# Centred rows for the first two token blocks of a sliding-attention and gMLP kernel

## The chip, the cores and the metric

The kernel runs on one core of a Trainium2 chip. A core has five engines, each with its own queue of instructions: TensorE (PE in the profile; its weight loads are PEld), VectorE (DVE), ScalarE (ACT), GpSimd (POOL) and SyncE (SP), which here only issues transfers. SP's, ScalarE's and GpSimd's queues issue DMAs; 16 DMA engines carry them out. The metric is the device time of one execution, in microseconds (us); the median of several runs counts.

## The reference

`x` holds 2048 tokens of 512 numbers. The rows are normalised once, `xn = (x - mean) / sqrt(var + 1e-5)`, and two mixers work on `xn`; their results are added to `x`.

```python
# A: dilated sliding attention, 32 heads of 16, window of 8 tokens, 2 apart
q, k, v = split(xn @ wqkv)
logits = einsum('bhsd,bhswd->bhsw', q, k[s - 2*w]) * 16**-0.5
a = softmax(logits) . v[s - 2*w] @ wo
# B: a gated MLP that mixes tokens
z = gelu(xn @ w_in)                       # 1792 wide
z1, z2 = z[..., :896], layernorm(z[..., 896:])
g = w_sp @ z2 + b_sp                      # w_sp: 2048 x 2048 over tokens
b = (z1 * g) @ w_out
return x + a + b
```

Types are bfloat16, with sums in float32.

## The kernel before

The tokens lie in 16 blocks of 128. A block has its tokens on the 128 partitions when it is loaded (`ldx`, tile `xin`, 8 slots), and its features on the partitions after it has been normalised and transposed (`xnT`), which is the form in which TensorE takes it as the stationary or the moving operand.

The work is a list of named tasks. A task is one or a few instructions on one engine, with the tiles that it reads and writes; from these the program derives the semaphore waits. The order of the tasks on each engine is not computed when the kernel is built: it is written out by hand in the five lists of `ORDERS` (line 206), and every engine runs its list strictly in order. A number behind a name is the token block, or the pair of blocks, or a group of columns.

How a block is made ready (`ln_block`, line 591):

- `bnst`, `bnag` (DVE, L595 and L598): mean and variance of the rows, from the loaded block.
- `rstd` (POOL, L600): variance to the power -0.5, a 128x1 operation.
- `norm` (DVE, L602): subtract the mean and multiply by `rstd`, written as `xn` in four slots.
- blocks 0 to 3: `xTr`, four 128x128 matmuls against the identity (PE, L619) into PSUM, and `xTe` (ACT, L633), which copies them to `xnT`. For block 0 the copy is split between ACT (`xTe0`, L625) and DVE (`xTf0`, L629).
- blocks 4 to 15: `xTd`, a transposing DMA on SP's queue (L606).

Before there is any work for it, TensorE runs filler matmuls on zeros: nine 128x512 ones (`warm`, L567), and two 128x320 ones behind xTr0 (`fill0`).

Then, on TensorE: `z2_b_h` (L815), the second half of `xn @ w_in` for block b, in two halves h of 448 columns (their weights are `w_in2a` and `w_in2b`, each loaded in two parts, one by SP's and one by ScalarE's queue); for blocks 0 to 3 it comes first of all. `z2g` (ACT, L826) is the gelu of a block, which also gives the sum of each row, and `z2s` (L834) the sum of squares; `zn` (L863, or L859 on ACT) normalises the block by them once four blocks are there. `Qj_c` and `Kj_c` (L669) are made for four blocks j at once, so that Q0_0 needs `xnT` of blocks 0 to 3 and the loaded weights `ldq`; K0_0 needs `ldk`; `V` (L646) needs `ldwv`. `QKe` and `Ve` (ACT) evacuate them.

The logits are products on DVE (`prod`, `padd`, L694 and L698, 128x4096 each), summed over the head's features on TensorE (`lg`, L707); the softmax follows, and later the products with V (`pv`, `pva`, `pvc`, L1000 to L1008). In between TensorE makes `z1` (L815). Then follow, for eight pairs of token blocks, the token mixing `w_sp @ z2` (`P1` to `P7`, L938; sums of weight blocks `S13`, `S2`, `S4` and of z2 blocks `T1` to `T4` on DVE save one product in eight), its evacuation, the gate `u` (DVE, L970), a transposing DMA of the result (`uT`, L980) and one of the attention's output (`OTd`, L1012), and the output product `out` (L1037 and L1041), which is added to x in PSUM, copied (`fin`) and stored (`st`).

PSUM has eight banks. Banks 0 to 5 go round in pairs through the products before the token mixing: a pair is written again when its evacuation is done.

The queue of SP begins with `ldx0 ldw_in2a_0 ldx2 ldw_in2b_0 ldx4 ldx5 ldx8 ldx6 ldx7 ldq ldx9 ldk ldx10 ldx11 ldwv xTd5`. Block 8 and those behind it are loaded into the slots of blocks 0 and on, so such a load waits until the old block has been read.

Of the kernel before, what the change touches and what calls it, by code (L numbers as in the profile page):

```python
# [14 lines left out]
class Plan:  # L15
# [183 lines left out]
ALU = mybir.AluOpType  # L199
# [8 lines left out]
warm xTr0 fill0 z2_0_0 xTr1 z2_0_1 z2_1_0 xTr2 z2_1_1 z2_2_0 xTr3 z2_2_1 z2_3_0 z2_3_1 Q0_0 Q0_1 K0_0 K0_1 K0_2  # L208
Q0_2 Q0_3 V0 V1 V2 V3 V6 K0_3 Q1_0 K1_0 V7 V4 V5 K1_3 Q1_3 Q1_1 Q1_2 K1_2 K1_1 z2_6_0 z2_6_1 z2_5_0 z2_4_1
z2_4_0 z2_5_1 lg0_0 z2_7_0 z2_7_1 V11 V10 V9 Q2_0 V8 K2_0 Q2_2 K2_1 Q2_1 K2_2 K2_3 Q2_3 z2_8_0 z2_8_1 z2_9_0  # L210
z2_10_0 z2_10_1 z2_9_1 z2_11_1 z2_11_0 V12 V13 lg1_0 Q3_0 K3_0 Q3_1 V14 K3_1 V15 K3_3 Q3_3 Q3_2 z2_12_1 K3_2
z2_14_1 z2_14_0 z2_12_0 z2_13_0 z2_13_1 lg2_0 z2_15_0 z2_15_1 z1_0_1 z1_2_0 z1_4_0 z1_4_1 z1_0_0 z1_2_1 z1_10_1
z1_6_1 z1_6_0 z1_8_1 z1_10_0 z1_8_0 z1_12_0 z1_12_1 z1_15_1 z1_15_0 z1_13_0 z1_13_1 z1_9_0 z1_9_1 lg3_0 z1_14_0
z1_7_0 z1_7_1 z1_14_1 z1_3_1 z1_1_1 z1_1_0 z1_11_1 z1_3_0 z1_11_0 P5_0 P1_1 z1_5_0 z1_5_1 P1_0 P5_1 P3_0 P6_0
P2_0 P7_0 P6_1 P4_0 P7_1 P2_1 P4_1 P1_2 P3_1 P2_2 P5_2 P6_2 P1_3 P3_2 P7_2 P2_3 P4_2 P6_3 P5_3 out0_0 P1_4 P7_3
P3_3 P4_3 P6_4 out2_0 P2_4 P5_4 P7_4 P3_4 P4_4 P1_5 out4_0 out6_0 P2_5 P1_6 P6_5 P5_5 P7_5 out8_0 out10_0 P3_5
P2_6 P5_6 P4_5 out12_0 out14_0 P6_6 P1_7 P3_6 P5_7 P7_6 P2_7 out15_0 P6_7 P4_6 P7_7 P3_7 out13_0 out11_0 P4_7
out9_0 out7_0 out5_0 out3_0 out1_0 out1_1
# [6 lines left out]
QKe3_0 QKe3_1 Ve15 Ve14 QKe3_3 z2s10 z2s11 QKe3_2 z2g14 z2g12 bspf z2g13 z2s12 z2g15 ldV0_0 lge2 z1g4 z1g0 z1g2
z2s13 z1g6 z2s14 z1g10 z2s15 z1g12 zm2 z1g15 z1g13 z1g8 lge3 z1g9 z1g7 z1g14 zn14 z1g1 zn13 z1g3 zn12 z1g11 zn15
S5_0 z1g5 fk_0 sexp0 fk_1 S2e_0 ldxr0 Sc_0 sln0 S3e_0 srec0 S2e_1 g11_0 g22_0 S5_1 g12_0 g21_0 S3e_1 g11_1 fk_2
sexp1 g21_1 Sc_1 S5_2 g22_1 S2e_2 os0_0 fk_3 sln1 ldxr2 Sc_2 S3e_2 g12_1 srec1 g21_2 os2_0 g11_2 S2e_3 S5_3
ldxr4 g22_2 ldV1_7 fin0_0 S3e_3 fk_4 g12_2 Sc_3 ldxr6 fin2_0 g11_3 S2e_4 g12_3 S5_4 g21_3 os4_0 st0_0 S3e_4
# [14 lines left out]
T1_1 zn10 T1_0 zn11 T3_0 S4_0 sm1_0 sm2_0 sm3_0 ssub0 S2_1 T3_1 T2_1 T2_0 T4_1 S4_1 sz1_0 sz2_0 sz3_0 T4_0 sm1_1
sm2_1 sm3_1 ssub1 h_0 sattn0 pv0 pv2 pva2048_0 S13_2 sz1_1 S2_2 sz2_1 h_1 pva1024_0 S4_2 pvc0 sz3_1 S13_3 u_0
S2_3 pv4 pv6 h_2 S4_3 sattn1 u_4 pva2048_1 S13_4 pva1024_1 S2_4 pvc1 S4_4 pv10 pv8 h_3 pva2048_2 pva1024_2 u_8
pvc2 S13_5 pv14 pv12 S2_5 pva2048_3 pva1024_3 h_4 pvc3 u_12 pv15 pv13 S4_5 pva2048_4 S13_6 pva1024_4 u_15 pvc4
h_5 pv11 pv9 S2_6 pva2048_5 pva1024_5 S4_6 pvc5 S13_7 pv5 S2_7 pv7 h_6 pva2048_6 u_11 pva1024_6 S4_7 pvc6 pv1
# [8 lines left out]
ldx13 Vw0 Vw1 Vw2 ldx12 ldx15 Vw3 xTd10 Vw7 xTd8 xTd9 Vw6 xTd11 Vw5 Vw4 ldw_in1 Vw8 xTd15 Vw10 xTd13 Vw11 xTd12  # L257
Vw9 xTd14 wT1_0 wT1_1 wT0_0 Vw12 Vw15 wT0_1 Vw14 Vw13 lgT1 lgT0 lgT3 lgT2 wT2_0 wT2_1 wT3_0 wT3_1 OTd0 uT_0
wT4_0 wT4_1 uT_2 uT_4 uT_6 wT5_0 OTd1 wT5_1 wT6_0 wT6_1 OTd2 uT_8 uT_10 OTd3 wT7_0 uT_14 uT_12 OTd4 wT7_1 uT_15
uT_13 OTd5 uT_11 OTd6 uT_9 uT_7 uT_5 uT_3 OTd7 uT_1 st1_0  # L260
# [6 lines left out]
    warm=9,  # L267
# [11 lines left out]
def build_kernel(nc, A_x, A_wqkv, A_wo, B_x, B_w_in, B_w_sp, B_b_sp, B_w_out, out,   # L279
# [49 lines left out]
    off["pb"] = base  # L329
    off["On"] = base  # L330
# [31 lines left out]
    with ExitStack() as es:  # L362
# [75 lines left out]
        for c in range(4):  # L438
# [749 lines left out]
```

## Time and profile before

| what | value |
|---|---|
| median of 3 runs | 226.94 us (226.94 to 227.38) |
| the profiled execution | 227.02 us, its span 225.2 us |
| TensorE busy | 220.5 us, 98% of the span |
| VectorE busy | 203.4 us, 90% |
| ScalarE busy | 148.5 us, 66% |
| GpSimd busy | 42.9 us, 19% |
| first useful matmul (`z2_0_0`) | 6.43 us after the span's start |
| Q and K begin | 13.69 us (first record) |
| last matmul ends | 222.9 us |

A line of the timeline gives the start, the duration of the merged group in us, the engine, the line of the kernel, the operation, its output and input, the count, and in brackets the idle time of the engine before the group and what ended it. A line of the groups gives the busy time and the mean duration of one instruction in ns. The time of an execution is the span and some 1.8 us around it.

### The profile page before, as it was taken

Reading aid. Unit: us, or ns where it says so; the run is one execution under the profiler, and the core shown is the slowest. Engines: PE = TensorE matmul, PEld = TensorE weight load, DVE = VectorE, ACT = ScalarE, POOL = GpSimd, SP = SyncE. Lnnn points to the kernel's source line nnn. Section 1 sums busy time; section 2 is a strip of 40 time slices with the busy share of each in tenths; the row PEclk is TensorE's granted clock in tenths of the full one; section 3 lists DMA queues with packets and bytes.
Section 4 is the critical chain, followed back from the end, with each engine's and each line's share of the span. In section 5 each row is a group of like instructions: output and inputs, shape, how many; then the busy total and the mean of one; then the engine's idle time right before and its main releaser. Section 6 shows DMA issues by size and latency. Waiting matters only on the chain.

```text
span 225.2 us, 3059 instructions
## 1 busy us (share of the span) xinstructions
PE 220.5 (98%) x1129; PEld 115.8 (51%) x1142; DVE 203.4 (90%) x208; ACT 148.5 (66%) x258; POOL 42.9 (19%) x40
## 2 busy tenths in 40 slices
PE   7999999999999999999999999999999999999995
PEld 3454454455454677665555554545454545544443
DVE  4879999999999999998699999999999999999700
ACT  2678767898969797897895686434525824546652
POOL 3438804990603205006000000000000000000000
DMA  6975536225925370451989189997898977347862
GB/s 207 347 191 86 173 74 171 111 71 135 232 80 140 89 260 0 91 98 43 237 120 212 45 173 160 302 236 181 172 129 238 182 159 137 96 111 175 189 148 70
DMA packets 84719, 34.18 MB, mean 152 GB/s; under 512 B 69232, under 2 KB 84352, under 8 KB 84704
## 3 DMA queue, kind: packets, MB, share of 16 engines
q1 hardware_dynamic: 74448, 23.77, 50.2%
q10 hardware_dynamic: 9376, 8.75, 13.2%
q0 software_dynamic: 880, 1.47, 2.4%
q8 instruction: 9, 0.15, 0.3%
q14 instruction: 6, 0.05, 0.1%
HBM read 12.98 MB, written 4.21 MB: 76 GB/s over the span
## 4 chain that ended last, share of the span: by engine, by line
PE 98%; issue 0%; DVE 0%
PE ps L938 38%; PE ps L815 22%; PE ps L669 12%; PE ps L1041 11%; PE ps L646 6%; PE ps L1037 6%; PE ps L567 2%; PE ps L707 1%; PE ps L619 0%; DVE arena L629 0%; DVE arena L1049 0%; DVE arena L493 0%; DVE fpool L494 0%
## 5 line engine op out<-in xcount | busy, mean ns | idle before, releaser
L938 PE MATMUL ps<-arena 128*128 128x448 bf16 x448 | 86.2, 352 | 0.0
L938 PEld LDWEIGHTS ps<-arena 128*128 128x128 bf16 x448 | 43.8, 98 | 41.3 <-ACT arena L944 0.4
L815 PE MATMUL ps<-arena 128*128 128x448 bf16 x256 | 50.8, 353 | 0.4 <-DVE arena L629 0.4
L815 PEld LDWEIGHTS ps<-arena 128*128 128x128 bf16 x256 | 30.2, 121 | 19.2 <-ACT arena L633 1.1
L694 DVE TENSOR_TENSOR arena<-arena 128x4096 bf16<-128x4096 bf16 x16 | 36.3, 2284 | 0.1
L1000 DVE TENSOR_TENSOR arena<-arena 128x4096 bf16<-128x4096 bf16 x16 | 36.1, 2288 | 0.1
L826 ACT ACTIVATE arena<-ps 128x896 bf16<-128x896 f32 x32 | 28.8, 915 | 7.7 <-PE ps L815 7.6
L669 PE MATMUL ps<-arena 128*128 128x512 bf16 x125 | 28.8, 379 | 0.2
L944 ACT ACTIVATE arena<-ps 128x448 bf16<-128x448 f32 x32 | 17.0, 542 | 17.7 <-PE ps L938 16.5
L1004 DVE TENSOR_TENSOR arena<-arena 128x4096 bf16<-128x4096 bf16 (+1 forms) x16 | 28.1, 1756 | 0.1
L600 POOL TENSOR_TENSOR fpool<-fpool 128x1 f32<-128x1 f32 x16 | 24.0, 1507 | 20.3 <-DVE fpool L598 19.3
L698 DVE TENSOR_TENSOR arena<-arena 128x4096 bf16<-128x4096 bf16 x12 | 27.4, 2285 | 0.1
L1041 PE MATMUL ps<-arena 128*128 128x512 bf16 (+2 forms) x117 | 26.9, 366 | 0.1
L1050 ACT ACTIVATE arena<-ps 128x512 bf16<-128x512 f32 (+1 forms) x16 | 9.5, 592 | 21.5 <-PE ps L1041 21.5
L669 PEld LDWEIGHTS ps<-arena 128*128 128x128 bf16 x128 | 14.4, 113 | 13.4 <-issue 0.4
L677 ACT ACTIVATE arena<-ps 128x1024 bf16<-128x1024 f32 x16 | 16.4, 1033 | 6.3 <-PE ps L669 6.2
L1041 PEld LDWEIGHTS ps<-arena 128*128 128x128 bf16 x119 | 11.4, 98 | 12.8
L851 POOL TENSOR_TENSOR fpool<-fpool 128x4 f32<-128x4 f32 x4 | 12.1, 3022 | 28.7 <-DVE fpool L848 28.7
L1037 PE MATMUL ps<-arena 128*128 128x512 bf16 (+2 forms) x62 | 15.3, 365 | 0.3
L834 ACT ACTIVATE arena<-arena 128x896 bf16<-128x896 bf16 x16 | 15.3, 954 | 0.1
L646 PE MATMUL ps<-arena 128*128 128x512 bf16 x62 | 14.5, 379 | 0.1
L595 DVE BATCH_NORM_STATS2 fpool<-arena 128x6 f32<-128x512 bf16 x16 | 10.6, 680 | 2.8 <-DMA arena<-in_A_x_dram 2.8
(76 smaller groups left out, 186.0 us busy)
## 6 DMA issues: line engine op xcount, KB each, us to landing
arena<-in_A_x_dram ACTq DMA_DIRECT2D x18, 128.0 KB, 2.8
vscr<-arena SPq DMA_DIRECT2D x16, 128.0 KB, 1.9
arena<-vscr ACTq DMA_DIRECT2D x1, 1920.0 KB, 9.0
out_dram<-arena ACTq DMA_DIRECT2D x15, 128.0 KB, 2.6
arena<-in_A_x_dram SPq DMA_DIRECT2D x14, 128.0 KB, 3.5
arena<-in_A_wqkv_dram SPq DMA_DIRECT2D x3, 512.0 KB, 5.0
arena<-vscr ACTq DMA_DIRECT2D x1, 1024.0 KB, 6.9
arena<-in_B_w_in_dram SPq DMA_DIRECT2D x1, 896.0 KB, 5.1
```

The lines of the kernel that those rows point to most:

```text
L600: T("pool", lambda g: g.tensor_tensor(Fv("rstd", 1, b), Fv("mv", 1, 2 * b + 1), Fv("mhalf", 1), ALU.pow), reads=[("mv", b), "mhalf"], writ ...
L646: last = t.matmul(bank(k + i), AC(off["xnT"] + dc * S + 128 * (b + i), [[1, 128]]), AC(off["wv_raw"] + 512 * dc, [[1, 512]]), start=(dc == ...
L669: last = t.matmul(bank(k + which), AC(off["wqk"] + 1024 * dc + col0, [[4, 128]]), AC(off["xnT"] + dc * S + 512 * j, [[1, 512]]), start=(dc ...
L694: T("dve", lambda v: v.tensor_tensor(pbv, qb, kb, ALU.mult), reads=[("QT", c, j), ("KT", c, j), ("KTpad", c, j)], writes=[("pb", s_)], est ...
L698: T("dve", lambda v: v.tensor_tensor(A("pb", 4096, 4096 * a), A("pb", 4096, 4096 * a), A("pb", 4096, 4096 * b), ALU.add), reads=[("pb", b) ...
L815: last = t.matmul(bank(k + hf, HF), AC(off["xnT"] + dc * S + t0, [[ts, 128]]), AC(off["w_in"] + 1792 * dc + c0, [[1, HF]]), start=(dc == 0 ...
L826: T("act", lambda a: a.activation(A(nm, FH, FH * b).rearrange("p (t n) -> p t n", t=2), PC(512 * k, [[512, 2], [1, HF]]), ACTF.Gelu_apprx_ ...
L938: last = t.matmul(bank(k, HF), AC(lo + 128 * s, [[1, 128]]), mov(s), start=(first and s == 0), stop=(s == 7), skip_group_check=True)
L1000: T("dve", (lambda iv, tv, av: lambda v: v.tensor_tensor(tv, iv, av, ALU.mult))(iv, tv, av), reads=[("attn", pairs[i][b]) for b in blks] + ...
L1004: T("dve", (lambda n: lambda v: v.tensor_tensor(AC(off["Vs"], [[4096, 2], [1, n]]), AC(off["Vs"], [[4096, 2], [1, n]]), AC(off["Vs"] + n, ...
L1037: t.matmul(po, AC(off["OT"] + 512 * os_ + 128 * cc, [[1, 128]]), AC(off["wo"] + 512 * cc + c0, [[1, n]]), start=False, stop=False, skip_gr ...
L1041: last = t.matmul(po, AC(off["uT"] + FH * us + 128 * fc, [[1, 128]]), AC(off["w_out"] + 512 * fc + c0, [[1, n]]), start=False, stop=(fc == ...
```

## The change

For token blocks 0 and 1, z2 is no longer computed from the normalised rows but from centred ones, `xc = x - mean`. The product of the weights with `xc` is multiplied by `rstd` inside the gelu instruction, whose scale operand is then the block's `rstd` (a number for each partition, that is, for each token).

- Block 0: `cen0` (DVE) subtracts the mean as soon as `bnag0` has given it. Block 1: `sum1` (ACT) computes minus the mean by an accumulating copy, and `cen1` (ACT) adds it, without DVE's statistics.
- `xTr0` and `xTr1` transpose `xc`, and `xTe0`, `xTf0`, `xTe1` copy it to a tile of its own, `xcT`. `xTr1` stands directly behind `xTr0` on TensorE, ahead of `fill0` and `z2_0_0`; the order behind that is z2_0_0, z2_1_0, z2_0_1.
- The full norms of blocks 0 and 1 (`norm0`, `norm1`) are still needed for Q, K, V and z1. They are transposed by two DMAs on SP's queue, `xTd0` and `xTd1`, which stand behind `ldx7`.
- `ldq` moves from SP's queue to ScalarE's, behind `xTe1`; `ldx8` moves behind `ldk`, which is behind `xTd1`.
- `warm` has eight matmuls instead of nine; `fill0` is 256 wide instead of 320.
- All five lists of `ORDERS` are new, to the end. They hold the same tasks as before but for those named.

```diff
     pe="""
-warm xTr0 fill0 z2_0_0 xTr1 z2_0_1 z2_1_0 xTr2 z2_1_1 z2_2_0 xTr3 z2_2_1 z2_3_0 z2_3_1 Q0_0 Q0_1 K0_0 K0_1 K0_2
-Q0_2 Q0_3 V0 V1 V2 V3 V6 K0_3 Q1_0 K1_0 V7 V4 V5 K1_3 Q1_3 Q1_1 Q1_2 K1_2 K1_1 z2_6_0 z2_6_1 z2_5_0 z2_4_1
...
+warm xTr0 xTr1 fill0 z2_0_0 z2_1_0 z2_0_1 xTr2 z2_1_1 z2_2_0 xTr3 z2_2_1 z2_3_0 z2_3_1 Q0_0 Q0_1 Q0_2 K0_0 K0_2
+K0_1 K0_3 Q0_3 V1 V2 V0 V3 V4 V7 Q1_0 V5 V6 K1_0 Q1_1 K1_1 Q1_3 K1_3 Q1_2 K1_2 z2_6_0 z2_4_1 z2_4_0 z2_5_0
...
     act="""
-actprime ldx1 ldw_in2a_1 ldw_in2b_1 ldx3 xTe0 xTe1 z2g0 xTe2 z2g1 xTe3 z2s0 z2g2 z2g3 QKe0_0 QKe0_1 halo0_0
...
+actprime ldx1 ldw_in2a_1 ldw_in2b_1 ldx3 sum1 cen1 xTe0 xTe1 ldq xTe2 z2g0 xTe3 z2g1 z2g2 z2g3 QKe0_0 halo0_0
...
     dve="""
-zeros steps0 steps1 bnst0 bnag0 bnst1 norm0 bnag1 xTf0 norm1 bnst2 bnag2 norm2 bnst3 bnag3 bnst5 bnag5 norm3
-bnst7 bnst6 bnst8 norm5 bnag6 bnst10 bnag7 bnst4 bnag10 bnst9 bnag4 zq0 bnst11 norm6 norm7 bnag8 prod0_0 norm4
...
+zeros steps0 steps1 bnst0 bnag0 cen0 bnst1 bnag1 xTf0 norm0 bnst2 bnag2 norm1 norm2 bnst3 bnag3 bnst5 bnag5
+norm3 bnst7 bnag7 bnst4 bnst6 norm5 bnst8 bnag4 bnag8 norm7 norm4 bnst9 bnag6 bnst11 bnag9 prod0_0 norm6 bnag11
...
     sp="""
-ldx0 ldw_in2a_0 ldx2 ldw_in2b_0 ldx4 ldx5 ldx8 ldx6 ldx7 ldq ldx9 ldk ldx10 ldx11 ldwv xTd5 xTd6 xTd7 ldx14 xTd4
...
+ldx0 ldw_in2a_0 ldx2 ldw_in2b_0 ldx4 ldx5 ldx6 ldx7 xTd0 xTd1 ldk ldx8 ldx9 ldx11 ldx10 ldwv xTd5 xTd7 ldx13
...
-    warm=9,
+    warm=8,
...
-        for which, eng in ((0, "sp"), (1, "sp")):
+        for which, eng in ((0, "act"), (1, "sp")):
...
+            if b < 2:
+                if b == 0:
+                    T("dve", lambda v: v.tensor_scalar(A("xc", 512, 512 * b), xin, Fv("mv", 1, 2 * b), None, ALU.subtract),
+                      reads=[("xin", xs_), ("mv", b)], writes=[("xc", b)], est=400, name="cen%d" % b)
+                else:
+                    T("act", lambda a: a.activation(A("xj", 512), xin, ACTF.Copy, scale=-1.0 / D, accum_out=Fv("nm", 1)),
+                      reads=[("xin", xs_)], writes=["xj", "nm"], est=c_act(512, accum=True), name="sum%d" % b)
+                    T("act", lambda a: a.activation(A("xc", 512, 512 * b), xin, ACTF.Identity, bias=Fv("nm", 1)),
+                      reads=[("xin", xs_), "nm"], writes=[("xc", b)], est=c_act(512), name="cen%d" % b)
...
+                T("pe", trc, reads=[("xc", b), "ident"], writes=[("ps", kk[0]), ("ps", kk[1])], est=430.0, name="xTr%d" % b)
...
+                if b == 1:
+                    filler(cfg["fill0"], "fill0", 107.0 * cfg["fill0"], reads=("zeros", ("xc", 1)), w=256)
             T("dve", lambda v: v.tensor_scalar(A("xn", 512, 512 * sl), xin, Fv("mv", 1, 2 * b),
                                                Fv("rstd", 1, b), ALU.subtract, ALU.mult),
               reads=[("xin", xs_), ("mv", b), ("rstd", b)], writes=[("xn", sl)], est=400, name="norm%d" % b)
-            if b >= XDMA:
+            if b >= XDMA or b < 2:
                 dma("sp", lambda e: e.dma_start_transpose(AC(off["xnT"] + 128 * b, [[S, 4], [1, 128]]),
...
-                        last = t.matmul(bank(k + hf, HF), AC(off["xnT"] + dc * S + t0, [[ts, 128]]),
+                        lhs = (A("xcT", 128, 512 * b + 128 * dc) if which and b < 2 else
+                               AC(off["xnT"] + dc * S + t0, [[ts, 128]]))
+                        last = t.matmul(bank(k + hf, HF), lhs,
...
             kw = dict(accum_out=Fv("s1", 1, b)) if which else {}
+            if which and b < 2:
+                kw["scale"] = Fv("rstd", 1, b)
```

More of the change, by code (lines that the diff above doesn't have):

```diff
@@ L213 @@
[L213 to L217, printed above, removed]
@@ L225 @@
[L225 to L229, printed above, removed]
@@ L244 @@
[L244 to L248, printed above, removed]
@@ new lines @@
+prod3_2 padd3_1 smask zq3 prod3_3 padd3_2 zn2 zv3 padd3_3 zn8 zn7 zn6 zn10 zn1 S13_0 zn9 S2_0 zn3 zn4 zn11 zm3
+zn5 T1_0 S4_0 T1_1 T3_0 S13_1 sm1_0 T2_0 sm2_0 sm3_0 ssub0 T3_1 T2_1 S2_1 T4_1 sz1_0 sz2_0 sz3_0 sm1_1 sm2_1
+S4_1 sm3_1 T4_0 h_0 ssub1 sattn0 pv0 pv2 sz1_1 pva2048_0 S13_2 S2_2 pva1024_0 S4_2 h_1 pvc0 sz2_1 u_0 pv4 S13_3
+sz3_1 S2_3 pv6 h_2 pva2048_1 u_4 pva1024_1 S4_3 pvc1 sattn1 S13_4 pv10 S2_4 pv8 h_3 pva2048_2 pva1024_2 S4_4
+pvc2 pv12 pv14 S13_5 u_8 u_12 S2_5 pva2048_3 S4_5 h_4 pva1024_3 pvc3 pv13 pv15 pva2048_4 pva1024_4 pvc4 S13_6
@@ L261 @@
+OTd4 uT_15 uT_13 uT_11 OTd5 OTd6 uT_9 uT_7 uT_5 OTd7 uT_3 uT_1 st1_0
 """.split(),
@@ L443, in build_kernel @@
         R1("wv_raw", "wv_raw", 2048)
-        R("xnT0a", "sb", [(off["xnT"] + dc * S, off["xnT"] + dc * S + 128) for dc in range(2)])
-        R("xnT0b", "sb", [(off["xnT"] + dc * S, off["xnT"] + dc * S + 128) for dc in range(2, 4)])
+        for b in range(2):
+            R1(("xc", b), "xc", 512, 512 * b)
+            for h in range(2):
+                R1(("xcT", b, h), "xcT", 256, 512 * b + 256 * h)
+        R1("xj", "xj", 512)
         for b in range(NB):
```

108 lines of the change are left out of this document (60 added, 48 removed).

## The prediction

> **What bounds the kernel now.** I read the page's engine table and chain first, then the timeline of TensorE, then that of all engines up to 22 us, then the groups by shape. The page:
>
> ```profile
> span 225.2 us, 3059 instructions
> ...
> PE 220.5 (98%) x1129; PEld 115.8 (51%) x1142; DVE 203.4 (90%) x208; ACT 148.5 (66%) x258; POOL 42.9 (19%) x40
> ...
> PE 98%; issue 0%; DVE 0%
> ```
>
> The chain is TensorE nearly alone; VectorE, at 90%, has little room behind it. The timeline of TensorE shows where useful work begins:
>
> ```profile
> 1.26 4.02 PE L567 MATMUL ps<-arena 128*128 128x512 bf16 x9 [1.26 <-DVE fpool L494]
> 5.07 0.63 PE L619 MATMUL ps<-arena 128*128 128x128 bf16 x4
> 5.50 0.51 PE L567 MATMUL ps<-arena 128*128 128x320 bf16 x2
> 6.43 0.92 PE L815 MATMUL ps<-arena 128*128 128x448 bf16 x4 [0.42 <-DVE arena L629]
> 7.19 0.39 PE L619 MATMUL ps<-arena 128*128 128x128 bf16 x4
> 7.41 1.78 PE L815 MATMUL ps<-arena 128*128 128x448 bf16 x8
> ...
> 13.69 5.99 PE L669 MATMUL ps<-arena 128*128 128x512 bf16 x27
> ```
>
> L567 is filler. Useful work starts at 6.43 (z2_0_0), and from there to 222.9 no matmul line has idle in front of it: a later stage can't become faster by this change, and the time moves only by what the stream before Q0_0 (L669) gains or what a new wait costs. What makes 6.43 is this, from the timeline of all engines:
>
> ```profile
> 2.90 0.69 DVE L595 BATCH_NORM_STATS2 fpool<-arena 128x6 f32<-128x512 bf16 x1 [1.49 <-DMA arena<-in_A_x_dram]
> 3.63 0.20 DVE L598 BATCH_NORM_AGGREGATE fpool<-fpool 128x2 f32<-128x9 f32 x1
> ...
> 3.91 0.58 POOL L600 TENSOR_TENSOR fpool<-fpool 128x1 f32<-128x1 f32 x1 [2.38 <-DVE fpool L598]
> ...
> 4.53 0.41 DVE L602 TENSOR_SCALAR arena<-arena,fpool 128x512 bf16<-128x512 bf16 x1
> ...
> 5.75 0.42 DVE L629 CAST arena<-ps 128x256 bf16<-128x256 f32 x1 [0.70 <-PE ps L619]
> ...
> 6.40 0.51 PEld L815 LDWEIGHTS ps<-arena 128*128 128x128 bf16 x4 [0.75 <-DMA arena<-in_B_w_in_dram]
> ```
>
> Statistics, the power on GpSimd (L600), norm, transposes, evacuation, first product. The last line names a load, but z2_0_0's own weights (w_in2a) were issued at 1.27 and 1.51 and took 3.7 and 4.2 us, so they were in by 5.71; the evacuation ended at 6.17, and 0.26 us of issue follows.
>
> **The change part by part.** (a) *Block 0's chain.* cen0 needs bnag0 only. It starts at 3.87 instead of norm0's 4.53 and, at L602's 0.41, ends at 4.28. xTr0 can't use all of it: filler matmuls start 0.43 apart, the ninth at 4.65. With eight, TensorE is free at 4.65, and xTr0 starts there instead of 5.07. From xTr0's start to the evacuation is 0.68 (5.07 to 5.75), so xTf0 runs 5.33 to 5.75, and with the same 0.26 z2_0_0 starts at 6.01: **0.42 gained**. Weights in at 5.71 are no bound, but leave only 0.04 before 5.75.
>
> (b) *Block 1's transposes leave the stream.* xTr1 holds it for 0.22 (7.19 to 7.41). Now it runs behind xTr0, at 5.08 to 5.5, where TensorE waits anyway. It needs cen1 by then: x1 was issued at 1.09 and took 2.1, so it lands at 3.2, when ScalarE has just issued its last load (2.50+0.49). sum1 costs the 0.60 of a 128x512 ACTIVATE plus 0.20 of accumulator read, cen1 0.60 plus 0.09 for its bias operand (L944 with and without it: 631 and 542 ns): 3.25+0.75+0.70 = 4.7, in time. **0.22 gained.**
>
> (c) Each pair behind a transpose waits for its evacuation: eight matmuls take 1.62 (chain, 7.57 to 9.19) where 8x0.189 is 1.51. z2_1_0 no longer does: xTe1 ends about 6.34, it starts at 6.77. **0.11 gained.** z2_0_1 now comes third, at 7.52; its weights (issued 2.0 and 2.23, 4.8 each) are in by 7.03.
>
> Sum: 0.75. The stream of before reaches Q0_0 at 13.48 (11.10 + 12x0.189 + 0.11; the row's 13.69 lacks one of 28 records), that of after at 12.72.
>
> (d) *xTr2 and xTr3* are wanted at 8.28 and 10.12. xTf0 ends 0.42 earlier; after it norm0, bnst2, bnag2, then 0.86 until norm2 (7.13 to 7.99 in before) give norm2 from 7.57 to 7.98, norm3 about 9.5 to 9.9. I take 0; norm1 now stands beside rstd2 on GpSimd, and were rstd2 delayed by all of it (0.4), 0.1 would be lost.
>
> (e) *SP's queue.* xTd0 and xTd1 stand behind ldx7. A transpose holds SP for 1.19 to 1.29 us (L606), and waits for its norm: xTd0 6.1 to 7.35, xTd1 to 8.6. Behind them: ldk (issued 7.32 before, now 8.6), ldx8 (4.97 before, now 9.05), ldx9, ldx11, ldx10, ldwv at about 10.7, as before. ldk at its own 6.2 us lands at 14.8; K0_0 comes fourth, at 12.72+3x0.865 = 15.3: covered, and without that cover it costs the difference. ldwv has until 19.6.
>
> (f) *ldq on ScalarE* takes about 0.45 of issue behind xTe1, at 6.34. Next on that engine is xTe2, not ready before 8.7, then z2g0: hidden. It took 5.0 us and is wanted at 12.72.
>
> (g) *New wait: Q0_0 on xTd0 and xTd1.* No row of before shows a transpose in this stretch, where the DMA share is 0.92 to 1.10 in each microsecond from 2.2 to 10. Lower bound: 2.4 (L606, quiet), landing 9.8, costing nothing; below nothing is excluded, for only a wait is added. Upper: ldk's 6.2, landing 13.6, costing 0.85. The nearest row is ldx9: issued 6.77, 128 KB, 5.3 us; x4 to x8, q and itself, 1.3 MB, had to land after 6.4, as x4 to x7, q and two transposes do now. From 7.36 that is 12.7: I take 0. The Trainium skill ("Trainium Kernel Development and Optimization", Key Constraints) says that queues of SP and ScalarE share the same 16 engines, so ldq's new queue buys issue time only; by it the 12.7 stands rather than some 10.5, and the price stays 0, but without cover.
>
> (h) *Elsewhere.* cen0 adds 0.41 to VectorE, where it waited for transposes (0.70) anyway. The first gelus pay 0.09 each for a scale operand; their banks are wanted at Q0_0 at the earliest, and z2g1 ends near 12.1. bnst8 now waits for x8 (before: landed 8.5). Issued 9.05 with 3.3 to 5.4 us, it comes 12.4 to 14.5; bnst8 to bnag9 fill 3.35 us, and prod0_0 can start only after QKe0_0, near 17.45 (17.32 before). So x8 has until 14.1, and lateness costs at most 0.4 at first. I take 0.
>
> (i) *The later orders.* Adding durations along the new lists (z2/z1 groups 0.757, Q/K/V 0.865, P 1.51; VectorE's 4096-wide ops 2.2 each) I looked for places where TensorE reaches work before VectorE has made it. lg3_0: behind prod0_0's 17.45 lie 28 such ops, 5 bnst x 0.65, 9 norms x 0.34, 2 zn x 0.42 and 14 small ones x 0.1, 70.3, and 0.4 by which the same sum on before falls short: padd3_3 ends 88.1. Ahead of lg3_0 lie 48 Q/K/V and 43 z groups and three lg of 0.55, 75.7 behind 12.72, and 0.15 as before falls short: wanted 88.6 (before: 88.1 and 90.3). P6_0: T2_1 ends 104.6, wanted 105.0 (105.2 and 107.2). out3_0: uT_3 in about 216, wanted 217.1. Nothing is late, but the room shrinks from 2 us to about 0.4. Price 0 if VectorE keeps time; each tenth beyond 0.4 is lost once, not at each place.
>
> The profiled execution took 227.02 (span 225.2, 1.8 around it), 0.08 above the median 226.94. 227.02-0.75 = 226.27, against the median 226.19; 0.1 for the joins of (d) and (g) gives **226.3**.
>
> **Rivals.** *1, slower: the transposes hold up Q0_0.* Place: TensorE before the first L669 group. It costs microsecond for microsecond from 12.72 on; the gain is gone at 13.5, and slower than can be told from no change at 13.9, 6.5 us after xTd1's issue. For it: no row has a transpose in a full DMA queue, and the 512 KB weight transposes (L900) took 4.1 to 7.0. Against: in quiet, a 128 KB one takes 2.4, and all loads issued between 5 and 9 us landed in 3.3 to 6.2. At 14.4 the time is 226.27+1.68 = 227.9.
>
> *2, the clock opens too late.* Filler matmuls run at half speed (512 columns in 0.43, later 448 in 0.189). The two of fill0 start at 5.50 and 5.71; 320 columns are 0.27 slow and 0.135 fast, so the speed changed near 5.65: 0.8 before z2_0_0, now only 0.36. If it changes at 7.0 in a run, the groups from 6.01 lose half of that, 0.5: 226.8. For it: one of three runs is 0.44 longer, which a change at 7.3 would make of the kernel before (half of 7.3-6.43). Against: the two others, and the profiled one. The Trainium skill ("TensorE: Matmul & The Clock Gate", Part 1) has the clock released after a busy window of about 3.4 us that runs freely, so that the moment differs from run to run; by it the change lies anywhere from 4.7 to 8.1 and the middle, 6.4, would make 226.45. The trace's 5.65 fits, but is one draw.
>
> *3, VectorE's room is used up.* x8 at 14.9 instead of 14.1, or as much lost in the waits of its new order: 0.8 late, less the 0.4, plus a tenth or two at other joins: 226.8. For: 90% busy, several places at 0.4 to 0.5. Against: in before sz1_0 waited 1.65 us for ScalarE's exp; in the new order only about 0.25, which gives 1.4 back from there on.
>
> **How the numbers follow.** 0.2% (0.45 us) is about what a measurement of this kernel can tell from no change. Forecast 226.3, own range 226.0 to 226.5: 0.55. Rival 2: 0.10. Rival 3: 0.10. Rival 1: 0.25. So faster 0.55, same 0.20, slower 0.25. The range runs from 226.0 (nothing lost, and a little more overlap at xTr2) to 227.8, which takes in rivals 2 and 3 and the milder half of 1, and leaves out about 0.2.
>
> **What would show it.** In the profile of after: z2_0_0's first matmul at 6.0 with three groups behind it unbroken (a, b, c); L669's first at 12.7 (sum); no idle before L669 released by a DMA (g); prod0_0 near 17.5 (h); no new idle before L707 or L938 (i). The prediction is wrong if cen1 ends after 5.1, if TensorE waits at Q0_0, or if idle appears in the middle, where the order and not the head decides.

## The result, and the profile after

The changed kernel takes 226.57 us (median of 22 runs; the middle half lies between 226.20 and 226.80), the kernel before 227.10 in the same comparison (22 runs, 226.93 to 227.37). The ratio is 0.9971, with a 95% interval of 0.9960 to 0.9983: 0.29% faster, or 0.66 us, where 0.28% had been forecast. One of the 22 runs, of 229.47 us, was slow as a whole, as was one of some 604 us in each of two series below; the ratios leave these out, and so do the medians and ranges further down. The means without it are 0.65 us apart, the two medians 0.53. The gain is over the 0.2% that can be told from no change, by little, and the interval starts at 0.17%.

The profiled execution of the changed kernel took 226.09 us (span 224.3, again 1.8 around it). That is among the shortest of its 22 runs, while the 227.02 of before lies in the middle of its own, so the 0.93 us between the two profiles is more than the gain of a usual run.

The timeline of TensorE, changed kernel (start, length, engine, line, operation, out<-in, count, and in brackets the idle before it and what ended it):

```profile
1.26 3.39 PE L573 MATMUL ps<-arena 128*128 128x512 bf16 x8 [1.26 <-DVE fpool L500]
4.49 0.39 PE L623 MATMUL ps<-arena 128*128 128x128 bf16 x4
5.05 0.40 PE L623 MATMUL ps<-arena 128*128 128x128 bf16 x4 [0.17 <-ACT arena L616]
5.28 0.38 PE L573 MATMUL ps<-arena 128*128 128x256 bf16 x2
5.78 2.43 PE L837 MATMUL ps<-arena 128*128 128x448 bf16 x12
8.05 0.39 PE L650 MATMUL ps<-arena 128*128 128x128 bf16 x4
...
12.56 7.07 PE L689 MATMUL ps<-arena 128*128 128x512 bf16 x32
```

z2_0_0 starts at 5.78 (6.43 before), three groups follow without a break (one, then xTr1, before), and Q0_0 starts at 12.56 (13.48 before). xTr1 (the second L623 row) waited 0.17 us for cen1, and nothing before L689 waited for a DMA. Here is what stands ahead of z2_0_0, from the timelines of VectorE and ScalarE:

```profile
3.95 0.35 DVE L611 TENSOR_SCALAR arena<-arena,fpool 128x512 bf16<-128x512 bf16 x1
5.05 0.38 DVE L630 CAST arena<-ps 128x256 bf16<-128x256 f32 x1
...
3.52 0.63 ACT L614 ACTIVATE arena<-arena 128x512 bf16<-128x512 bf16 x1 [1.20 <-DMA arena<-in_A_x_dram]
4.27 0.72 ACT L616 ACTIVATE arena<-arena,fpool 128x512 bf16<-128x512 bf16 x1
```

cen0 ends at 4.30 and xTf0 at 5.43. The second part of z2's first weights (w_in2a, issued at 1.51 on ScalarE's queue, 4.2 us to landing) came at 5.71, just ahead of 5.78: in this execution the evacuation is no longer the last to arrive. In a second profile of the same kernel it is again (the table below).

The rest of the kernel is the same length: from Q0_0 to the end of the execution it is 226.09-12.56 = 213.53 us, and 227.02-13.48 = 213.54 before. The change acts on the head alone, as the prediction had it.

One more place matters later: lg3_0, where TensorE meets VectorE's padd3_3 (timelines of VectorE and TensorE, changed kernel):

```profile
86.23 2.28 DVE L718 TENSOR_TENSOR arena<-arena 128x4096 bf16<-128x4096 bf16 x1
88.44 0.93 DVE L887 TENSOR_SCALAR arena<-arena,fpool 128x896 bf16<-128x896 bf16 x2
...
88.67 0.61 PE L727 MATMUL ps<-arena 128*32 128x512 bf16 x8
```

VectorE's next operation starts at 88.44, so padd3_3 was done about then, 0.23 us ahead of lg3_0.

### The profile page after: what moved, and what is told of

The parts are those of the page before. It is cut to its first block, busy times and chain, and to the rows that moved or that the text cites. A ratio compares the mean times of both kernels' runs of the same rounds, so it can differ in the third digit from the quotient of the medians.

```text
span 224.3 us, 3083 instructions
## 1 busy us (share of the span) xinstructions
PE 220.5 (98%) x1141; PEld 115.4 (51%) x1141; DVE 203.5 (91%) x209; ACT 149.7 (67%) x261; POOL 38.2 (17%) x40
## 4 chain that ended last, share of the span: by engine, by line
PE 96%; DVE 1%; DMA 1%; issue 0%
PE ps L962 38%; PE ps L837 22%; PE ps L689 12%; PE ps L1065 11%; PE ps L1061 6%; PE ps L666 6%; PE ps L727 1%; DMA arena<-in_A_x_dram 1%; DVE fpool L601 1%; PE ps L650 0%; DVE fpool L604 0%; DVE arena L611 0%; DVE arena L637 0%; DVE arena L630 0%; DVE arena L1073 0%
## 5 line engine op out<-in xcount | busy, mean ns | idle before, releaser
L850 ACT ACTIVATE arena<-ps 128x896 bf16<-128x896 f32 x30 | 27.0, 917 | 6.1 <-PE ps L837 6.1
L689 PE MATMUL ps<-arena 128*128 128x512 bf16 x128 | 29.5, 379 | 0.0
L1065 PE MATMUL ps<-arena 128*128 128x512 bf16 (+2 forms) x119 | 27.0, 366 | 0.0
L606 POOL TENSOR_TENSOR fpool<-fpool 128x1 f32<-128x1 f32 x16 | 21.2, 1332 | 15.3 <-DVE fpool L604 15.1
L689 PEld LDWEIGHTS ps<-arena 128*128 128x128 bf16 x128 | 14.3, 114 | 13.7 <-issue 0.7
L875 POOL TENSOR_TENSOR fpool<-fpool 128x4 f32<-128x4 f32 x4 | 10.3, 2568 | 38.9 <-DVE fpool L872 38.9
L1061 PE MATMUL ps<-arena 128*128 128x512 bf16 (+2 forms) x68 | 16.6, 366 | 0.0
L666 PE MATMUL ps<-arena 128*128 128x512 bf16 x64 | 15.1, 379 | 0.0
L968 ACT ACTIVATE arena<-ps,fpool 128x448 bf16<-128x448 f32 x16 | 9.9, 631 | 7.6 <-PE ps L962 4.3
```

The costliest lines, as they stand in the source:

```text
L666: last = t.matmul(bank(k + i), AC(off["xnT"] + dc * S + 128 * (b + i), [[1, 128]]), AC(off["wv_raw"] + 512 * dc, [[1, 512]]), start=(dc == ...
L689: last = t.matmul(bank(k + which), AC(off["wqk"] + 1024 * dc + col0, [[4, 128]]), AC(off["xnT"] + dc * S + 512 * j, [[1, 512]]), start=(dc ...
L850: T("act", lambda a: a.activation(A(nm, FH, FH * b).rearrange("p (t n) -> p t n", t=2), PC(512 * k, [[512, 2], [1, HF]]), ACTF.Gelu_apprx_ ...
L968: T("act", lambda a: a.activation(dst, bank(k, HF), ACTF.Identity, **kw), reads=[("ps", k), "bspf"], writes=[key], est=est, name="%s_%d" % ...
L1061: t.matmul(po, AC(off["OT"] + 512 * os_ + 128 * cc, [[1, 128]]), AC(off["wo"] + 512 * cc + c0, [[1, n]]), start=False, stop=False, skip_gr ...
L1065: last = t.matmul(po, AC(off["uT"] + FH * us + 128 * fc, [[1, 128]]), AC(off["w_out"] + 512 * fc + c0, [[1, n]]), start=False, stop=(fc == ...
```

## The experiments

All edits are made to the changed kernel. The kernel before ran along in each of the three series, with medians of 227.05, 227.00 and 227.04. The changed kernel itself has two medians, 226.57 above and 226.29 in the second series, so a difference of 0.3 us between kernels of different series says little.

### What is left if block 1 is as before

```diff
-warm xTr0 xTr1 fill0 z2_0_0 z2_1_0 z2_0_1 xTr2 z2_1_1 ...
+warm xTr0 fill0 z2_0_0 xTr1 z2_0_1 z2_1_0 xTr2 z2_1_1 ...
-            if b < 2:
+            if b < 1:
```

(the same for the five other conditions on `b < 2`; sum1, cen1 and xTd1 go, xTe1 returns to its old form, norm1 stands ahead of norm0 on VectorE, and fill0 is 320 wide again, behind xTr0)

> Block 1 goes back: it is normalised, transposed in the stream behind z2_0_0 and copied to xnT as before; only block 0 is centred. Head theory (the gain is what the stream before Q0_0 gains): z2_0_0 still starts at 5.8 to 6.0, but xTr1 holds the stream for 0.22 again and the pair behind it waits 0.1 for its evacuation, so Q0_0 comes 0.3 later after z2_0_0 than in the changed kernel (7.1 instead of 6.8 us), and the time is 0.3 above the changed kernel's, 0.35 under the kernel before. Rival (the gain comes from the new orders further on, or from block 0 alone): no later than the changed kernel.

Measured: 227.27 us (11 runs, 226.85 to 229.15), ratio 1.0015 [0.9992, 1.0038]. It should have been 0.3 above the changed kernel and was 0.7 above. (The next expectation has 227.43 and 0.86, which count all twelve runs.) This series has no profile of a usual run, so the kernel was run once more.

> The kernel with block 0 alone centred once more, for its profile: it was 0.86 above the changed kernel (227.43 against 226.57), where 0.3 was expected. Theory: z2_0_1 comes second there, right behind z2_0_0 and xTr1, and its weights w_in2b are not in by then (they land 6.8 to 8.3, and it is wanted at 6.8 to 7.0), so TensorE waits for that load at z2_0_1; with block 1 ready early the second place is taken by z2_1_0, which needs w_in2a alone. The profile then shows idle before L837 released by a load of w_in ahead of the second group of four, 0.2 to 1.3 us of it. Rival: the wait is at the next transposes (xTr2 waiting for norm2), with none for a load.

Measured: one execution of 227.16 us. The timeline of TensorE:

```profile
5.07 0.74 PE L573 MATMUL ps<-arena 128*128 128x320 bf16 x2
6.17 1.26 PE L837 MATMUL ps<-arena 128*128 128x448 bf16 x4 [0.36 <-DMA arena<-in_B_w_in_dram]
7.27 0.39 PE L650 MATMUL ps<-arena 128*128 128x128 bf16 x4
7.50 1.78 PE L837 MATMUL ps<-arena 128*128 128x448 bf16 x8
...
13.56 7.07 PE L689 MATMUL ps<-arena 128*128 128x512 bf16 x32
```

The theory named a wait of z2_0_1 for its weights, the rival one of xTr2. There is neither. Instead z2_0_0 waited 0.36 us for the weights of the first half, which landed only at 6.1, and its four matmuls took 1.10 us up to xTr1 (7.27-6.17) instead of the 0.76 of a group at full speed: the clock opened inside them, that is, the matmuls went over to twice the speed (at 6.88 by the trace's clock record, which the table below uses). From z2_0_0 to Q0_0 are 7.39 us; less the 0.34 for the clock they are 7.05, which is what the kernel before has (13.48-6.43). With block 1 centred too, the same stretch is 6.78. So block 1's part of the change is worth 0.27 us, whatever the start, and block 0's part is all in the start, where weights and clock can take it back. That explains this execution; why two of the eleven runs took 228.93 and 229.15 stays open, as no such execution was profiled.

### The transposes that Q0_0 waits for

```diff
-... ldx6 ldx7 xTd0 xTd1 ldk ldx8 ldx9 ...
+... ldx6 ldx7 ldk xTd0 xTd1 ldx8 ldx9 ...
```

> ldk is issued ahead of xTd0 and xTd1 on SP's queue; both transposes are still issued at the same moment, for norm0 is what xTd0 waits for. In the changed kernel xTd1 landed at 12.4, 0.15 before Q0_0 at 12.56. Theory that the new wait is covered by only a tenth or two and that a transpose queues behind the bytes ahead of it: xTd1 lands about 1.5 us later (512 KB at some 340 GB/s), near 13.9, Q0_0 starts near 13.9 and the time is 1.2 to 1.4 above the changed kernel's, 0.6 above before. Rival (a transfer between SBUF places is not held up by loads from HBM ahead of it): xTd1 within 0.3 of 12.4 and the same time as the changed kernel.

Measured: 228.21 us (middle half 227.76 to 228.80), ratio 1.0045 [1.0023, 1.0067]. TensorE:

```profile
6.51 1.67 PE L837 MATMUL ps<-arena 128*128 128x448 bf16 x8 [0.68 <-DMA arena<-in_B_w_in_dram]
8.48 0.92 PE L837 MATMUL ps<-arena 128*128 128x448 bf16 x4 [0.30 <-DMA arena<-in_B_w_in_dram]
...
15.61 5.56 PE L689 MATMUL ps<-arena 128*128 128x512 bf16 x25 [1.69 <-DMA arena<-arena]
```

xTd0 and xTd1 were issued at 6.1 and 8.3, took 8.7 and 6.9 us, and Q0_0 waited 1.69 us for them. In the changed kernel they were issued at 5.78 and 7.07, took 6.2 and 5.3, and landed at 12.0 and 12.4, 0.16 us ahead of Q0_0. Not all of that is the edit's: xTd1 went out 1.2 us later because norm1 stands behind bnst2 on VectorE, which waited 1.05 us for x2, and this execution (228.93) is one of the slower of its series. But xTd0, issued at 6.1 as in most of the others, landed at 14.8 and would have held Q0_0 until then alone, and the median is 1.64 above the changed kernel's, where 1.2 to 1.4 was expected. So the wait of the prediction's first rival is real, and a second 512 KB load ahead of the transposes, besides q's, is enough to turn the change into a loss.

```diff
-        for which, eng in ((0, "act"), (1, "sp")):
+        for which, eng in ((0, "sp"), (1, "sp")):
```

(and ldq in SP's order between ldx7 and xTd0, out of ScalarE's)

> ldq goes back to SP's queue, behind ldx7 and ahead of xTd0. Theory that the queue of ldq matters for nothing but issue time, because all queues share the DMA engines: ldq lands 0.5 to 1.5 earlier, xTd1 lands within 0.4 of where the changed kernel has it (12.4), the time is within 0.2 of the changed kernel's. Rival (a transpose overtakes ldq only if ldq is on another queue): xTd1 lands 1 us or more later, Q0_0 waits for it, and the time is 0.8 to 1.2 above the changed kernel's.

Measured: 226.52 us (middle half 226.30 to 226.81), ratio 0.9988 [0.9967, 1.0010]; the interval is wide because of a single run of 229.08. By the median it is 0.23 above the changed kernel run again in the same series (226.29, below), within what runs of one kernel differ by. In the profile xTd0 and xTd1 were issued at 6.1 and 7.4 and took only 4.6 and 3.8 us: they landed at 10.7 and 11.2, earlier than with q on ScalarE's queue, where later was feared. So ldq's queue is neither a gain nor a loss that can be measured here. The Trainium skill ("Trainium Kernel Development and Optimization", Key Constraints) says that the queues share the same engines; that the time hardly moves with the queue agrees with it.

### VectorE's room

Three places for ldx8, which bnst8 and so all of VectorE's later order wait for. Early and a little late:

```diff
-... xTd0 xTd1 ldk ldx8 ldx9 ldx11 ldx10 ldwv ...
+... xTd0 xTd1 ldx8 ldk ldx9 ldx11 ldx10 ldwv ...     (early)
+... xTd0 xTd1 ldk ldx9 ldx11 ldx10 ldx8 ldwv ...     (late)
+... xTd0 xTd1 ldk ldx9 ldx11 ldx10 ldwv ldx8 ...     (last)
```

> ldx8 ahead of ldk instead of behind it. In the changed kernel VectorE waited 1.96 us for x8 (13.0 to 14.9), prod0_0 started at 18.05 and padd3_3 ended at 88.5, just when lg3_0 was wanted. Theory that VectorE's lag is nearly all within the room left: prod0_0 starts at 17.4 to 17.5, padd3_3 ends about 0.6 earlier, TensorE's stretch from Q0_0 to out1_0 (206.9 us) shrinks by 0.1 at most, the time is the same or 0.1 lower. Rival (the late x8 costs what VectorE waits): 0.6 or more lower.

Measured: 226.67 us, ratio 0.9978 [0.9964, 0.9992]. prod0_0 waited 1.69 us for ScalarE (QKe0_0) instead of VectorE's own work, and the time is that of the changed kernel: x8's lateness there (it landed near 14.9) costs nothing that can be measured.

> ldx8 behind ldx10, three loads later. x8 lands about 16 instead of 14.9, prod0_0 starts near 19.1. Theory that the room behind prod0_0 is used up at 18.05 and that each further tenth is lost once: lg3_0 waits about 1.0 us for padd3_3, TensorE's stretch from Q0_0 to out1_0 grows from 206.9 to about 207.9, the time is 0.9 to 1.1 above the changed kernel's. Rival (the orders have the 2 us of room of the kernel before): no change of time.

Measured: 226.73 us, ratio 0.9976 [0.9962, 0.9990]. No loss either, but the test was weak: x8 landed at 15.5, only 0.6 later, and in the profiled execution the clock opened late, so that Q0_0 was 0.7 later as well and VectorE stood no worse against TensorE than before. Hence the third place:

> ldx8 issued behind ldwv, at about 11.1 instead of 9.05 (nothing else moved). It lands 4 to 6 us later, at 15.1 to 17; bnst8 to bnag9 (3.35 us) stand ahead of prod0_0, which starts at 18.5 to 20.4 instead of 17.3 to 18.05. If VectorE's room in the later orders is about 0.4 us (step i of the prediction; padd3_3 ended 88.44 and lg3_0 began 88.67 in the changed kernel's profile), all of the lag beyond that is lost once, at lg3_0 at the latest: 0.4 to 2.0 us above the changed kernel, 226.8 to 228.4, with idle in front of L727. If there is more room than that (VectorE waits elsewhere give it back): 226.2 to 226.5, and padd3_3 no later than 88.5.

Measured: 228.13 us (4 runs, 227.90 to 228.53), ratio 1.0049 [1.0036, 1.0062]. From the timelines of VectorE and TensorE:

```profile
17.03 0.69 DVE L601 BATCH_NORM_STATS2 fpool<-arena 128x6 f32<-128x512 bf16 x1 [4.16 <-DMA arena<-in_A_x_dram]
20.18 2.25 DVE L714 TENSOR_TENSOR arena<-arena 128x4096 bf16<-128x4096 bf16 x1
88.36 2.29 DVE L718 TENSOR_TENSOR arena<-arena 128x4096 bf16<-128x4096 bf16 x1
90.56 0.93 DVE L887 TENSOR_SCALAR arena<-arena,fpool 128x896 bf16<-128x896 bf16 x2
...
12.87 7.07 PE L689 MATMUL ps<-arena 128*128 128x512 bf16 x32
29.41 5.37 PE L689 MATMUL ps<-arena 128*128 128x512 bf16 x24 [0.48 <-ACT arena L672]
90.70 0.62 PE L727 MATMUL ps<-arena 128*32 128x512 bf16 x8 [0.48 <-DVE arena L718]
```

Counted from Q0_0, prod0_0 starts 7.31 us later (5.49 in the changed kernel) and padd3_3 is done 77.69 later (75.88): a lag of 1.8 us passes through all of VectorE's order and nothing is given back on the way. From Q0_0 to lg3_0 are 77.83 us instead of 76.11, 1.72 more, and the time after Q0_0 is 228.13-12.87 = 215.26 instead of 213.53, 1.73 more. So it is lost once, by lg3_0, and not again. Not all of it is lost at lg3_0 itself, which waits 0.5; by the starts of the rows between, 1.18 us are gone before lg0_0 (44.37 against 42.88, less the 0.31 between the Q0_0 starts), around the V, Q and K groups of blocks 4 to 7. Of these, 0.33 are lost at Q1_0, and their way can be followed: norm6, behind bnst8 in VectorE's order, starts at 22.34 (20.21 in the changed kernel), its transpose is issued at 22.8 and takes 2.5 us, and Q1_0's weight load is recorded as released by a transposing DMA at 25.28. Most of the rest lies around the one wait that TensorE's rows record there, 0.48 for ScalarE's evacuation of V (L672); that this goes back to the late norms too is argued from the order, not shown. I had named only lg3_0.

### Weights and clock: what sets the start

The first half of z2's weights cut 3 to 1 between SP's and ScalarE's queue instead of 2 to 2 (and the second half 1 to 3):

```diff
...
-        ld_win_h("w_in2a", FH, HF, 2)
-        ld_win_h("w_in2b", FH + HF, HF, 2)
+        ld_win_h("w_in2a", FH, HF, 3)
+        ld_win_h("w_in2b", FH + HF, HF, 1)
```

> w_in2a is cut three parts on SP's queue to one on ScalarE's (two to two in the changed kernel), w_in2b one to three; bytes and number of loads are the same. In the profiles so far z2_0_0 starts at 5.78, 5.96, 6.51 and 6.79 where w_in2a's second part lands at 5.7, 5.8, 6.4 and 6.7. Theory that this load now decides when z2_0_0 starts in most executions: both parts are in 0.3 to 0.4 us earlier, z2_0_0 starts at 5.5 to 6.0, the median is 0.2 to 0.4 under the changed kernel's 226.57 and the runs lie closer together. Rival (the spread of the changed kernel comes from the moment the clock opens, and the load is in time): same median, same spread.

The changed kernel once more, in the same series:

> The changed kernel itself, on the chip of the three above, for another profile and as their reference. Theory that the head alone sets the time: the profiled time is Q0_0's start plus 213.3 to 213.5 (226.09 and 12.56 in the first profile), whenever Q0_0 starts; its start follows w_in2a's landing and the moment the clock opens. Rival: another place takes part, and the difference is off by more than 0.3. The median is 226.4 to 226.7.

Measured: 226.34 us with the cut (middle half 226.13 to 226.62), ratio 0.9969 [0.9957, 0.9981], and 226.29 for the changed kernel (11 runs, 226.12 to 226.71), ratio 0.9971 [0.9959, 0.9984]. The cut narrows the spread if anything; it doesn't move the median. In the changed kernel's second profile the weights were in by 5.6 and TensorE waited 0.23 us for the evacuation (L630) ahead of z2_0_0, at 5.87: there neither weights nor clock set the start. In the profile of the cut both parts of the weights were in by 5.6, but the clock opened late: the 12 matmuls from z2_0_0 on took 2.67 us to xTr2 (5.96 to 8.63) instead of 2.27. With the weights in time, the clock was next.

One filler matmul at the start instead of eight:

```diff
-    warm=8,
+    warm=1,
```

> One filler matmul at the start instead of eight. If the clock opens some 3.1 to 5.8 us after sustained matmuls began (4.33 to 7.1 in the profiles so far, the first filler at 1.26), it now opens that long after xTr0's start near 4.4, at 7.5 to 10.2: the z2 groups run at half speed from 5.9 on, half of the stretch is lost, 0.8 to 2.1 us: Q0_0 at 13.4 to 14.7, time 227.2 to 228.5. If the clock opens at a time of its own, whatever TensorE does: no loss, Q0_0 near 12.6, time 226.2 to 226.5.

Measured: 227.48 us (8 runs, 227.03 to 228.50), ratio 1.0022 [1.0005, 1.0038]. The profiled execution (227.03), first TensorE's matmuls, then the weight loads for them (PEld):

```profile
4.30 1.23 PE L623 MATMUL ps<-arena 128*128 128x128 bf16 x8 [2.43 <-DVE arena L611]
5.32 0.64 PE L573 MATMUL ps<-arena 128*128 128x256 bf16 x2
5.74 3.47 PE L837 MATMUL ps<-arena 128*128 128x448 bf16 x12
9.05 0.39 PE L650 MATMUL ps<-arena 128*128 128x128 bf16 x4
13.49 7.07 PE L689 MATMUL ps<-arena 128*128 128x512 bf16 x32
...
7.24 0.15 PEld L837 LDWEIGHTS ps<-arena 128*128 128x128 bf16 x1 [0.22 <-issue]
7.61 0.15 PEld L837 LDWEIGHTS ps<-arena 128*128 128x128 bf16 x1 [0.22 <-issue]
7.92 0.85 PEld L837 LDWEIGHTS ps<-arena 128*128 128x128 bf16 x5 [0.16 <-issue]
```

The weight loads are 0.37 us apart, double the 0.189 of a 448-column matmul, until 7.61, and then no more: the speed changed near 7.8. The 12 matmuls took 3.31 us to xTr2, 1.04 more than 2.27, and half of 7.8-5.74 is 1.03. This bears out the prediction's price for a late clock (half of the lateness after z2_0_0) with a moment read independently of the loss. The rival, a clock that opens at a time of its own, gave 226.2 to 226.5; none of the eight runs is below 227.03. The change comes 3.5 us after matmuls began in earnest at 4.30; in the nine kernels with eight fillers for which the trace has the moment, it came 2.8 to 5.9 us after the first filler at 1.26. The Trainium skill ("TensorE: Matmul & The Clock Gate", Part 1) has the clock released after a busy window of about 3.4 us that runs freely. The spread of 3.1 us is near the width of such a window, but the two shortest, 2.8 and 3.1, are less than a whole one, and there the measurement decides. The 1.5 us between the shortest and the longest of the eight runs are near 1.7, half of such a window, an estimate from that page's figure.

### Together

The cut of the weights and q on SP's queue in one kernel:

> Two edits of the changed kernel together: the first half of z2's weights cut 3/1 between the two load queues instead of 2/2 (and the second half 1/3), and q's load moved from ScalarE's queue to SP's, between ldx7 and xTd0. My theory: only the start of Q0_0 counts (profiled time minus that start was 213.3 to 213.6 in eight profiles), and it is set by the landing of the first half of z2's weights and by the moment at which the clock opens. The split makes the weights land near 5.6 instead of 5.5 to 6.7, q on SP lets xTd1 land near 11.2 instead of 12.4: the median stays at 226.2 to 226.4, ratio 0.9965 to 0.9975, with less spread than the changed kernel (quartiles within 0.35). Rival, the DMA traffic ahead of Q0_0 sets it (two transposes behind one more load): Q0_0 released by a DMA, 226.8 or more.

Measured: 226.47 us (middle half 226.18 to 226.92), ratio 0.9979 [0.9965, 0.9993]. Faster than the kernel before, and not to be told from the changed one. The spread did not get smaller, against the expectation. Its profile shows what both edits buy and that it is not enough: z2_0_0 at 5.74, after a wait of 0.20 for the weights, Q0_0 at 12.56 as in the changed kernel. Another 0.11 went at z2_0_1, which waited for the second half of the weights (in at 7.3). It also shows VectorE with more room: x8 in by 14.3, prod0_0 at 17.46, and padd3_3 done at 87.86 where lg3_0 starts at 88.67 (timelines of VectorE and TensorE):

```profile
17.46 2.25 DVE L714 TENSOR_TENSOR arena<-arena 128x4096 bf16<-128x4096 bf16 x1
85.65 2.28 DVE L718 TENSOR_TENSOR arena<-arena 128x4096 bf16<-128x4096 bf16 x1
87.86 1.35 DVE L887 TENSOR_SCALAR arena<-arena,fpool 128x896 bf16<-128x896 bf16 x3
...
88.67 0.62 PE L727 MATMUL ps<-arena 128*32 128x512 bf16 x8
```

No kernel of this study beats the changed one by more than its own two medians differ.

### All profiles side by side

Landing is that of the later part of the first half of z2's weights (issue at 1.51 plus its time to landing). "Clock" is the first entry, full clock, of the clock record kept in the trace; two profiles have none. "12 matmuls" is from z2_0_0 to xTr2, where the three groups stand together. Where the profile lacks the first record of Q0_0 (31 or 25 of 32 in the row), 0.216 (a quarter of a 0.865 group) is taken off and the value marked *. The last column is the time of the profiled execution less Q0_0's start.

| kernel | weights in | clock | z2_0_0 | 12 matmuls | Q0_0 | time after Q0_0 |
|---|---|---|---|---|---|---|
| before | 5.71 | - | 6.43 | - | 13.48 | 213.54 |
| changed | 5.71 | 4.31 | 5.78 | 2.27 | 12.56 | 213.53 |
| changed, again | 5.6 | - | 5.87 | 2.27 | 12.58 | 213.54 |
| x8 early | 6.7 | 6.85 | 6.79 | 2.28 | 13.51* | 213.55 |
| x8 late | 5.8 | 7.18 | 5.96 | 2.86 | 13.26* | 213.54 |
| x8 last | 6.0 | 6.24 | 6.11 | 2.31 | 12.87 | 215.26 |
| q on SP | 5.5 | 5.71 | 5.96 | 2.26 | 12.67 | 213.51 |
| weights cut | 5.6 | 6.79 | 5.96 | 2.67 | 13.07 | 213.55 |
| cut, q on SP | 5.6 | 4.08 | 5.74 | 2.38 | 12.56 | 213.62 |
| one filler | 5.3 | 7.84 | 5.74 | 3.31 | 13.49 | 213.54 |
| block 0 only | 6.1 | 6.88 | 6.17 | - | 13.56 | 213.60 |
| transposes behind ldk | 6.4 | 5.38 | 6.51 | 2.73 | 15.39* | 213.54 |

Except with x8 last, where VectorE is held up, the time after Q0_0 is 213.5 to 213.6: the head alone decides. Wherever the clock opened behind z2_0_0, half of the difference is what the matmuls lost, to 0.03 us (x8 late 0.61 and 0.59, weights cut 0.42 and 0.40, one filler 1.05 and 1.04, block 0 only 0.35 and 0.34). The excess of the last row, 0.46, and that of "cut, q on SP", 0.11, are no matter of the clock: z2_0_1 waited there for the second half of the weights, which came at 8.3 and 7.3. The three kernels that move only ldx8 differ from the changed one behind 8.4 us, too late to touch weights or clock, so with the two profiles of the changed kernel itself they are five draws of the same head. Their Q0_0 starts are 12.56, 12.58, 12.87, 13.26 and 13.51. The middle one gives 213.54+12.87 = 226.41, near the measured 226.57 and 226.29, and the ends, 226.1 and 227.05, take in the middle half of the runs. In one draw the clock is late (7.18), in one the weights (6.7) and the clock (6.85) are.

## Why the prediction was right, step by step

**(a) Block 0's chain, 0.42.** Measured 0.65 in the profile (6.43 to 5.78). In this execution the start was better by 0.23: the clock opened at 4.31 instead of near 5.65, so the last filler was short and xTr0 began at 4.49, not 4.65, its transposes ran at full speed, and xTf0 ended at 5.43 instead of 5.75. The step that was wrong is "weights in at 5.71 are no bound". It took one landing of one execution as fixed. In twelve profiles the weights landed between 5.3 and 6.7, and in four of them a wait for them is recorded right before z2_0_0 (0.68, 0.66, 0.36, 0.20). Before the change the evacuation, done at 6.17 and 0.26 of issue behind it, covered most of that spread. The change removed the cover together with the cost. The weights are not the only limit, though. Of the eleven profiles with block 0 centred they came last in six, and the evacuation in one (0.23 of waiting, z2_0_0 at 5.87). In the other four z2_0_0 follows fill0 with no idle recorded. In three of these it starts at 5.96, where 6.01 was predicted: xTf0 was done at 5.74 (5.75 predicted), and with the clock still slow, in two of them, the fillers end only just before it as well. In the kernel with one filler the fillers alone hold it: xTf0 was done at 5.37, the weights were in at 5.3, and fill0 runs from 5.32 to z2_0_0 at 5.74. The prediction does not count fill0 as a limit; a shorter one was not tried.

**(b) and (c), 0.22 and 0.11.** Measured together 0.27: the stretch from z2_0_0 to Q0_0 shrank from 7.05 to 6.78, and the kernel with block 0 alone has 7.05 again when its clock loss is taken off. The missing 0.06 is the join at Q0_0 (12.56 where the twelve matmuls behind xTr3's last group end at 12.49). cen1 ended at 4.99 instead of 4.7, because x1 landed 0.3 later than before; 5.1 was the limit given.

**(d), (f).** Right. No idle is recorded in front of xTr2 and xTr3, and ldq on ScalarE cost nothing that the kernel with q on SP gets back (226.52 against 226.29).

**(e)** Right: ldk was issued at 8.42 and landed near 14.5 (at most 14.8 was said); no wait of K0_0.

**(g) The new wait, priced at 0.** Right, with the value taken from ldx9: 12.7 was estimated, 12.4 came. Its cover was 0.16 us, and the kernel with the transposes behind ldk shows what lies beyond: 1.69 of waiting. The first rival's mechanism and its price were right, its condition was not met: microsecond for microsecond from 12.72 on, Q0_0 at 15.39 gives 226.27+2.67 = 228.94, and that execution took 228.93.

**(h), (i) VectorE.** The condition of the third rival was met in the first profile: x8 came at 14.9, 0.8 late. (In the second profile of the same kernel it was in by 14.1, and prod0_0 started at 17.29.) Its price was not paid. prod0_0 slid by 0.6, from 17.45 to 18.05, and the room was larger than the 0.4 given: in the combined kernel, where prod0_0 starts at the predicted 17.46, padd3_3 is done at 87.86 (88.1 was predicted) and lg3_0 starts at 88.67 (88.6). From the kernel with x8 last, the join itself takes 0.14, so the room was 0.67, and the changed kernel's first profile uses all of it but 0.09. "Each tenth beyond is lost once" is shown by that kernel: a lag of 1.8 cost 1.73.

**The second rival, the late clock.** It is no alternative to the forecast: the gain and a late clock occur together. It was priced rightly (half of the lateness) and it happened, for 0.34 to 0.59 us, in three of the ten profiles of changed kernels with eight fillers (block 0 only, x8 late, weights cut). The two profiles of the changed kernel itself happened to have it in time (4.31, and near 5.0 by the distance of its matmuls).

**The sum.** The dense sum of 0.75 was too small for a run in which all goes well (0.93), and such runs are not the usual ones. Some 0.3 of it is taken back on average, which leaves the 0.66 measured; that weights, fillers and clock take it is shown for the profiles in the table, and inferred for the runs that were only timed. That the forecast, 0.64 against the median it was given, comes so near owes something to these two errors of opposite sign.

## What to carry to other kernels

When a change shortens the critical chain of the head, list everything that used to arrive during the time saved, and treat each arrival as a spread, not as the one number of the one profile: here weights landing at 5.3 to 6.7 us and a clock opening at 4.1 to 7.2, which the old chain, with its first product at 6.43, had covered in good part, became the limit in many executions. Find the first instruction behind which the stream is dense and subtract its start from the time of each execution; a constant remainder (213.5 here, in eleven of twelve profiles) says that a single number tells the whole effect. And price a new wait by the nearest transfer in the same traffic, then move the transfer once to see how thin the cover is.

## What the runs showed of the hardware

The granted clock as the profile's views print it does not show the half-speed phase. In the kernel with one filler, the windows of TensorE at half speed and after it read the same (window, sum, busy time and count of PE, granted clock, DMA share, GB/s):

```profile
6.90:7.30 0.40, 0.40 (x3) 1.00 1.08 376
8.10:8.50 0.40, 0.40 (x4) 1.00 0.88 264
```

The clock record kept in the trace (`clock` of core 0, less the start of the first instruction) begins with an entry of full clock at 7.84 in this run; before its first entry it has none, and the view prints 1.00 there. The distance of the matmuls gives the same moments: near 7.8 with one filler, near 4.33 in the changed kernel (4.31 in the record), near 7.1 in the one with x8 late (5.96+2x0.59; 7.18 in the record), and 5.65 in the kernel before, whose trace has no entry.

A DMA transpose of 128 KB inside the chip took 2.4 us in a quiet stretch of the kernel before, 2.8 us in the head of the kernel with block 0 alone, which has a single one, and with two 3.8 to 6.7 us, or 6.9 and 8.7 behind ldk. The same 224 KB load of weights, issued at 1.51 each time, took 3.8 to 5.2 us in the ten profiles where it has that size, a spread larger than what the change is worth.
